# The late phases of a three-part kernel: sums of experts by accumulating DMAs, decode in whole slices, another TensorE order

## The chip, the core and the metric

One core of one Trainium2 chip. The metric is the device time of one execution in microseconds (us), the median of the runs. A core has TensorE (PE, its weight loads PEld), VectorE (DVE), ScalarE (ACT), GpSimd (POOL) and SyncE (SP), each with an instruction queue of its own that runs in order; DMAs are issued from such a queue and carried out by 16 DMA engines.

## The reference

```python
def _attn_ref(q, k, v, alpha):          # 4 batches, 8 heads, 768 steps, head width 48
    for t in range(S):
        state = alpha[:, :, t, :, None] * state + np.einsum('bhd,bhe->bhde', k[:, :, t], v[:, :, t])
        y[:, :, t] = np.einsum('bhd,bhde->bhe', q[:, :, t], state)

def _moe_ref(x, domain_probs, w1, w2):  # 3072 tokens, width 384, 4 experts of 1024
    p = domain_probs / (domain_probs.sum(-1, keepdims=True) + 1e-09)
    for e in range(E):
        h = np.maximum(x @ w1[e], 0.0)
        out += p[:, e:e + 1] * (h @ w2[e])

def _moe2_ref(x, w_in, w_out):          # hidden width 2048
    h = x @ w_in
    g = h * np.clip(h + 3.0, 0.0, 6.0) / 6.0
    return g @ w_out
```

The three run one after the other, the output of each being the x of the next. `w_in` and `w_out` arrive as 64-bit floats; everything else is 32-bit.

## The kernel before

Tokens stand in six blocks of 512 (`NB`). Matrices are held as a high and a low part in fp32r, so each product is three matmuls: high weight x high data, low x high, high x low.

**First stage, to about 460 us.** The recurrence, with the first seven weight slices (`S0` = 7, a slice is 256 columns of the hidden width) of the experts done beside it for all six blocks: all of expert 0 and three quarters of expert 1. Each block's sum for either expert is multiplied by its probability and stored in DRAM as `acc_d[0]` or `acc_d[1]`. The change leaves this stage alone; its last block ends as the "tail" (L1797).

**Second and third stage, from about 518 us.** The other nine expert slices, then the eight slices of the last layer. Here two blocks (a pair, y = 0 and 1) are worked together, and the first layer of a slice is a fast matrix product of 2 x 3 by 3 x 2 blocks in 11 products instead of 12. A *group* is one slice for one pair: 11 products (M0 to M10) and 12 second-layer units (four h tiles, `o_` = 0 to 3, by three output parts m; y = `o_` % 2). Each product and unit is three matmuls of 128x512. There are 27 groups in the second stage and 24 in the third. A *segment* is the run of groups of one expert (or of the last layer) for one pair; at its end the six sums leave PSUM. The expert segments of a pair are of 1, 4 and 4 slices, so there are nine segment ends in the second stage.

The products run in two PSUM banks. `chain_a` takes M9, M5, M0, M7, M6 in turn, `chain_b` M10, M4, M2, M3, M8, M1. Each adds to what the bank holds, and between two additions the sum so far is taken out: ScalarE copies chain_a (`ct`, add_copy, L1544), VectorE adds the copy to chain_b (`cs`, add_sum, L1552), and the gate makes an h pair (`hh`, `hl`, add_gate) of it: two steps in the second stage (L1569, L1572), four in the third (L1578 to L1583). The next product into a bank waits until that has been read: M5 and M0 and M7 for `ct`, M2, M8 and the next group's M10 for `cs`, the next M9 for the gate that reads chain_a.

**What runs beside.**
- x: `add_x` loads a pair's blocks, GpSimd forms differences (L1365 to L1379), ScalarE and VectorE split them into high and low (`X..h` L1391, `X..l` L1396).
- Weights: `add_w`; on a slice's first use two DMAs for the first layer (`f_r0`, L1443) and one for the second, GpSimd forms sums (L1463 to L1466), ScalarE casts (L1473, L1479, L1486), VectorE subtracts (L1475, L1481, L1488); the result is stored in `ws_d` and loaded from there for the other pairs.
- Decode of the 64-bit weights: `add_decode`, 48 pieces of 256 columns, 24 of `w_out` first and then 24 of `w_in`: load `draw`, VectorE L1311, ScalarE L1312, VectorE L1313 to L1325, GpSimd's add L1326, a store into `w_out32` or `w_in32`. Slices of the last layer are then loaded from these.
- Sums of experts: at a pair's first segment end VectorE multiplies the PSUM sums by the probabilities into SBUF tiles `acc` (L1675); at later ends into `o` (L1687), and GpSimd adds `o` to `acc` (L1688). GpSimd also adds what the first stage left (`acc_d[0]` and `acc_d[1]`, loaded as `xr`, L1643). When the pair is done `acc` is stored as `x2_d`, the x of the third stage.
- The end: VectorE transposes the six sums (L1712), and each is written to `out` by four DMAs of 64 KB (L1718), 18 from SP and 6 from ACT for the last pair.

**What sets the order.** All operations of the late stages are written as entries of a list, with an engine, a planned duration, a `lag` until others may use the result, and dependencies (`op`, `dma`, `dve`, `act`, `pool`, `pe_op`). TensorE's entries keep the order in which they are written. `schedule()` works due times back from them, plays the list forward, and so puts the entries of every other engine in a fixed order. That order is what is built: an engine then waits at each instruction for its semaphores, and everything behind it in its queue waits too. `Ring` objects hand out buffers in turn; who wants a buffer waits for the users of its previous content.

## Time and profile before

| | |
|---|---|
| median of 3 runs | 1354.7 us (1353.49 to 1355.38) |
| profiled execution | 1354.69 us, its span 1353.0 us, mean TensorE clock 0.991 |
| TensorE matmul busy | 1311.8 us (97% of the span) |
| VectorE, ScalarE, GpSimd busy | 981.4, 593.9, 266.2 us |
| HBM read and written | 167.69 and 70.30 MB |
| GpSimd's sums of experts (L1643, L1688) and decode adds (L1326) | 24, 36 and 48 instructions |

The span runs from the program's first instruction to its last; the profiled execution's own time is 1.7 us longer. Busy time of TensorE is modelled, since matmuls overlap, so the number of matmuls started in a stretch says more than the busy share. Names in rows are those of the program without buffer numbers: out<-in. A line is a line of the kernel before; after the change the same operations stand some 20 to 30 lines further down.

### The profile page before, as it was taken

The page shows a single profiled execution, that of the slowest core. Times are in us where ns is not written, and L with a number is a line of the kernel's source. Part 1 is how long each engine was busy: PE and PEld are TensorE (multiplying, and loading weights), DVE is VectorE, ACT ScalarE, POOL GpSimd, SP SyncE. Part 2 cuts the span into 40 slices and gives each one's busy share as a digit, 9 for nine tenths or more (in the row PEclk, how much of TensorE's full clock was granted, in tenths as well). Part 3 has the DMA queues.
Part 4 walks back from the last instruction along what each step waited for, and adds up shares of the span by engine and source line. Part 5 has one row for each costly group of instructions (what it writes and reads, how often), then busy time and mean ns, then how long its engine had stood idle before and what let it go on. Part 6 is the DMA issues. An engine that isn't in the chain of part 4 may idle for free.

```text
span 1353.0 us, 27179 instructions
## 1 busy us (share of the span) xinstructions
PE 1311.8 (97%) x10877; PEld 1087.1 (80%) x10877; DVE 981.4 (73%) x1771; ACT 593.9 (44%) x1097; POOL 266.2 (20%) x288
## 2 busy tenths in 40 slices
PE   8899999999999999989999999999999999999996
PEld 7789887888888888767877887888788888888885
DVE  8899977777875354888898879887886574455443
ACT  4655455444444233533433333334555554444442
POOL 4000000000000131448355424452540010000000
PEclk8899999999999999999999999999999999999998
DMA  7765545436252453877787678865564474446423
GB/s 205 202 169 143 166 111 144 139 95 188 76 146 64 129 195 109 281 261 266 266 288 255 201 228 277 276 215 213 195 241 159 140 202 143 145 130 166 136 74 47
DMA packets 173709, 239.76 MB, mean 177 GB/s; under 512 B 74000, under 2 KB 143504, under 8 KB 167056
## 3 DMA queue, kind: packets, MB, share of 16 engines
q1 hardware_dynamic: 170272, 237.45, 56.0%
q8 instruction: 85, 1.39, 0.4%
q10 hardware_dynamic: 3312, 0.59, 0.3%
q14 instruction: 40, 0.33, 0.1%
HBM read 167.69 MB, written 70.30 MB: 176 GB/s over the span
## 4 chain that ended last, share of the span: by engine, by line
PE 77%; DVE 9%; DMA 4%; ACT 3%; POOL 3%; issue 2%; SPq 0%; ACTq 0%; DVEq 0%; POOLq 0%
PE sum L1619 24%; PE chain_b L1534 12%; PE ph L923 12%; PE chain_a L1534 10%; PE po L969 9%; PE po L1797 2%; PE py L628 2%; PE pa L525 1%; DMA wr<-in_moe_w_dram 1%; PE py L650 1%; DMA w_out<-da 1%; PE pu L573 1%; POOL acc L1688 1%; DVE dhc L1311 1%; POOL acc L1643 1%
## 5 line engine op out<-in xcount | busy, mean ns | idle before, releaser
L1619 PE MATMUL sum<-hh,V 128*128 128x512 f32 x1224 | 377.9, 390 | 0.0
L1619 PEld LDWEIGHTS sum<-hh,V 128*128 128x128 f32 x1224 | 230.5, 188 | 48.0
L1619 PE MATMUL sum<-hl,V 128*128 128x512 f32 x612 | 238.8, 390 | 0.2 <-DVE hl L1572 0.2
L1552 DVE TENSOR_TENSOR cs<-ct,chain_b 128x512 f32<-128x512 f32 x153 | 104.6, 684 | 90.0 <-PE chain_b L1534 65.4
L1544 ACT COPY ct<-chain_a 128x512 f32<-128x512 f32 x153 | 89.5, 585 | 130.5 <-PE chain_a L1534 130.0
L1619 PEld LDWEIGHTS sum<-hl,V 128*128 128x128 f32 x612 | 115.2, 188 | 25.2 <-DVE hl L1572 0.6
L933 ACT ACTIVATE hh<-ph 128x512 fp32r<-128x512 f32 (+1 forms) x98 | 52.5, 538 | 173.9 <-PE ph L923 172.5
L937 DVE SCALAR_TENSOR_TENSOR hl<-ph,hh 128x512 fp32r<-128x512 f32 (+1 forms) x98 | 59.7, 611 | 68.1 <-ACT hh L933 67.8
L1583 DVE SCALAR_TENSOR_TENSOR hl<-g,hh 128x512 fp32r<-128x512 f32 x96 | 68.1, 709 | 55.7 <-ACT hh L1580 55.4
L1569 ACT ACTIVATE hh<-cs 128x512 fp32r<-128x512 f32 x81 | 51.2, 632 | 128.4 <-DVE cs L1552 128.3
L1370 POOL TENSOR_TENSOR pu<-room 128x256 f32<-128x256 f32 x2 | 1.6, 787 | 455.8 <-DVE X00l L1396 453.2
L969 PE MATMUL po<-hh,w1h 128*128 128x512 f32 (+1 forms) x249 | 90.5, 371 | 0.0
L1578 ACT ACTIVATE g<-cs,three 128x512 f32<-128x512 f32 x72 | 52.1, 724 | 79.7 <-DVE cs L1552 79.6
L969 PE MATMUL po<-hh,w1l 128*128 128x512 f32 (+1 forms) x249 | 86.4, 355 | 0.0
L1572 DVE SCALAR_TENSOR_TENSOR hl<-cs,hh 128x512 fp32r<-128x512 f32 x81 | 76.0, 939 | 13.8 <-ACT hh L1569 13.5
L969 PE MATMUL po<-hl,w1h 128*128 128x512 f32 (+1 forms) x249 | 80.6, 355 | 3.2 <-DVE hl L937 3.2
L923 PE MATMUL ph<-xh,w0h 128*128 128x512 f32 (+1 forms) x294 | 77.8, 374 | 2.7 <-ACT xh L893 1.2
L1580 ACT ACTIVATE hh<-g 128x512 fp32r<-128x512 f32 x96 | 60.8, 633 | 37.3 <-DVE g L1579 37.0
L1579 DVE SCALAR_TENSOR_TENSOR g<-g,cs 128x512 f32<-128x512 f32 x72 | 52.9, 735 | 33.2 <-ACT g L1578 33.1
L923 PE MATMUL ph<-xh,w0l 128*128 128x512 f32 (+1 forms) x294 | 74.6, 363 | 0.0
L923 PE MATMUL ph<-xl,w0h 128*128 128x512 f32 (+1 forms) x294 | 74.5, 362 | 0.0
L1326 POOL TENSOR_TENSOR da<-da,dhc 128x256 f32<-128x256 f32 x48 | 40.9, 852 | 167.9 <-DVE dhc L1325 106.9
(315 smaller groups left out, 2797.8 us busy)
## 6 DMA issues: line engine op xcount, KB each, us to landing
V<-ws_d SPq DMA_DIRECT2D x34, 1280.0 KB
V<-ws_d SPq DMA_DIRECT2D x34, 768.0 KB
ws_d<-V SPq DMA_DIRECT2D x17, 1280.0 KB
ws_d<-V SPq DMA_DIRECT2D x17, 768.0 KB
vl<-vd SPq DMA_DIRECT2D x96, 96.0 KB
xr<-acc_d SPq DMA_DIRECT2D x24, 384.0 KB
xr<-x_d SPq DMA_DIRECT2D x20, 384.0 KB
draw<-in_moe_w_out_dram SPq DMA_DIRECT2D x24, 256.0 KB
```

What stands on the lines that cost most here:

```text
L923: pe.matmul(ph[:, 0:n], w[:, j, fs], x[:, j, cs], start=(o == 0 and j == 0), stop=(o == 2 and j == KT - 1),)
L933: high = lambda: nc.scalar.activation(hh[:, 0:n], ph[:, 0:n], AF.Relu)
L937: nc.vector.scalar_tensor_tensor(hl[:, 0:n], ph[:, 0:n], 0.0, hh[:, 0:n].bitcast(F32), op0=ALU.max, op1=sub)
L969: pe.matmul(accs[vi][m][:, 0:n], w[:, z, ms], h[:, 0:n], **fl)
L1534: pe.matmul(chain[bank], a, b, start=first_ and o == 0, stop=o == 2, skip_group_check=True)
L1544: o = act(512, lambda: nc.scalar.copy(CR.place(k), chain[0]), dep, d)
L1552: o = dve(512, lambda: nc.vector.tensor_tensor(SR.place(k), CR[kc], chain[1], op=add), dep, oc, d)
L1572: lambda: nc.vector.scalar_tensor_tensor(HR[k][1], get(), 0.0, HR[k][0].bitcast(F32), op0=ALU.max, op1=sub),
L1579: b = dve(512, lambda: nc.vector.scalar_tensor_tensor(GR[kg], GR[kg], 6.0, get(), op0=ALU.min, op1=mul), a)
L1580: hh = act(512, lambda: nc.scalar.activation(HR.place(k)[0], GR[kg], AF.Copy, scale=1.0 / 6.0), b, d)
L1583: lambda: nc.vector.scalar_tensor_tensor(HR[k][1], GR[kg], 1.0 / 6.0, HR[k][0].bitcast(F32), op0=mul, op1=sub),
L1619: pe.matmul(bank[(y, m)], a, b, start=first_ and x == 0, stop=last_ and x == 2, skip_group_check=True)
```

## The change

1. **Sums of experts by DMA.** The tiles `acc` and GpSimd's adds go. Every segment end multiplies into `o`, and GpSimd issues a DMA that adds `o` to `acc_d[0]` in DRAM (54 of 256 KB). `acc_d[1]` is added to `acc_d[0]` block by block by six DMAs from DRAM to DRAM. `x2_d` is now `acc_d[0]` itself.
2. **Decode in whole slices.** 16 pieces of 768 columns, `w_in` and `w_out` of a slice in turn, one buffer each, the add on VectorE, the result stored in the layout in which the weights are wanted (`w32_d`). Each piece has a latest time (`cap`), 24.5 us apart.
3. **TensorE's order.** The second-layer units wait in a list, at least nine TensorE entries after their gate, and are dealt out in ones, twos and threes between the products (`seconds`).
4. **Four h pairs** instead of three (`HR`), the third of them in the pool that opens after the tail.
5. **Reserves in the list.** Entries marked `soft` (preparation of x and weights, decode, DMAs) are planned as if their inputs came later by `SOFT`: 0.2 us behind PE, 0.5 behind DVE and ACT, 1.5 behind POOL, 3 behind a DMA. The two loads of `f_r0` become one entry.
6. **Last block in halves.** In the last group the y = 0 units go first, and the last three units, of y = 1, are done in halves of 256 tokens, each with its own transposes and writes (4 writes of 32 KB instead of one set of 64 KB); of the y = 1 writes ACT issues every second one.

```diff
+    SOFT = dict(PE=200, DVE=500, ACT=500, POOL=1500, SP=3000, ON=0)
...
+    def lag(o, n_):
+        if n_.eng == o.eng and o.eng != "SP":
+            return 0
+        return o.lag + (SOFT[o.eng] if n_.soft else 0)
...
-                (n_.due - (o.lag if n_.eng != o.eng or o.eng == "SP" else 0) for n_ in o.next), default=pos + 60000
+                (n_.due - lag(o, n_) for n_ in o.next), default=pos + 60000
             ) - o.dur
-            o.due = d if o.due is None else min(o.due, d)
+            c = o.cap[0].due + o.cap[1] if isinstance(o.cap, tuple) else o.cap
+            o.due = min(x for x in (o.due, d, c) if x is not None)
...
+    w32_d = dram.tile([2 * NS2, P, 3 * SL], F32, name="w32_d")
+    x2_d = acc_d[0]
...
+    HPOOLS = (hp, hp, None, late_pool)
     HR = Ring(
-        lambda k: [(late_pool if k % 3 == 2 else hp).tile([P, 512], F32R, tag=z, name=f"{z}_{k}") for z in ("hh", "hl")], 3
+        lambda k: [(HPOOLS[k % 4] or more).tile([P, 512], F32R, tag=z, name=f"{z}_{k}") for z in ("hh", "hl")], 4
     )
...
-    AC = Ring(named("acc", [P, KT, NB], bufs=2), 2)
...
-        CW = 256
-        RAW = Ring(named("draw", [P, CW, 2], I32, bufs=2), 2)
...
+        CW = 3 * SL
+        RAW = Ring(named("draw", [P, CW, 2], I32), 1)
+        HC, SQ, A_ = (Ring(named(z, [P, CW]), 1) for z in ("dhc", "dsq", "da"))
+        for s_, y in [(s_, y) for s_ in range(NS2) for y in range(2)]:
...
-            o9 = op("POOL", 850, lambda a=a, hc=hc: nc.gpsimd.tensor_tensor(a(), a(), hc(), op=add), o8)
-            o10 = dma(350, 128, lambda a=a, d_=d_, c=c: nc.sync.dma_start(d_[:, CW * c : CW * (c + 1)], a()), o9)
+            o9 = dve(CW, lambda a=a, hc=hc: ve.tensor_tensor(a(), a(), hc(), op=add), o8, soft=True)
+            o10 = dma(350, 384, lambda a=a, x=2 * s_ + y: nc.sync.dma_start(w32_d[x], a()), o9)
...
+            for o in (o1, o2, o3, o4, o5, o6, o7, o8, o9, o10):
+                o.cap = 150000 + 24500 * (2 * s_ + y + 1)
...
-        l0 = [dma(900, 256, lambda: f_r0(0), da, dec0, later)]
-        if ph == 1:
-            l0.append(dma(500, 128, lambda: f_r0(1), da, l0[0], later))
+        l0 = [dma(1300, 384, lambda: [f_r0(x) for x in range(3 - ph)], da, dec0, later)]
...
+    def seconds(n):
+
+        nonlocal clock
+        for _ in range(n):
+            if units and units[0][0] <= clock:
+                add_unit(*units.pop(0)[1:])
+                clock += 1
+
+    def pool_dma(fn, *deps):
+
+        o = op("POOL", 1200, fn, *deps, soft=True)
+        o.lag = 5000
+        return o
+
+    def add_acc(pr, deps):
         for y in range(2):
...
+            t0 = (2 * pr + y) * NB
+            merged[2 * pr + y] = [pool_dma(lambda t0=t0, e=e: nc.gpsimd.dma_start(
+                acc_d[0][:, :, t0 : t0 + NB], acc_d[e][:, :, t0 : t0 + NB], accum_op=add), deps) for e in range(1, EP)]
...
-            o2 = pool(512, lambda: nc.gpsimd.tensor_tensor(AC[ka][:, m], AC[ka][:, m], OR[k], op=add), o1, writes[m])
+            o2 = pool_dma(lambda: nc.gpsimd.dma_start(
+                acc_d[0][:, m, b * NB : b * NB + NB], OR[k], accum_op=add), o1, merged[b])
             OR.use(k, o1, o2)
...
+        add_product(G, "M9", free_a)
+        a1 = add_copy(G, pe_last)
+        seconds(2)
         add_product(G, "M10", free_b)
+        add_product(G, "M4")
+        s0 = add_sum(G, a1, pe_last)
+        add_gate(G, 0, *s0)
+        seconds(1)
+        add_product(G, "M5", a1[1])
+        a2 = add_copy(G, pe_last)
...
+        seconds(3)
+        add_product(G, "M0", a2[1])
+        a3 = add_copy(G, pe_last)
...
+            seconds(1)
+            s3 = part_b()
+            seconds(1)
+            part_a()
...
+        seconds(2)
         add_product(G, "M8", s3[1])
+        add_product(G, "M1")
...
+        if end:
+            units.sort(key=lambda u: u[2] % 2)
+            for u in units[:-KT]:
+                add_unit(*u[1:])
+            for half in range(2):
+                for u in units[-KT:]:
+                    add_unit(*u[1:], half)
+        else:
+            seconds(2)
```

`part_b` is M2, M3, their sum and its gate, `part_a` M7, M6 and the gate that reads chain_a; before, the order was M9, M10, M4, three units, M5, M2, M3, M0, three units, M7, M6, three units, M8, M1, three units.

**Place one: TensorE, the products M5 and M0 (X12 and X14) in a group of the third stage.** `X..h` and `X..l` are the parts of x, `V..` a slice's weights, `sum` the second-layer banks. Before:

```order
L1534 MATMUL chain_a_7821<-X12h_3_12920,V00_16_13972 128x512 x2
L1534 MATMUL chain_a_7821<-X12l_3_12930,V00_16_13972 128x512
L1534 MATMUL chain_b_7822<-X17h_3_12923,V00_16_13972 128x512 x2
L1534 MATMUL chain_b_7822<-X17l_3_12935,V00_16_13972 128x512
L1534 MATMUL chain_b_7822<-X13h_3_12996,V00_16_13972 128x512 x2
L1534 MATMUL chain_b_7822<-X13l_3_13005,V00_16_13972 128x512
L1534 MATMUL chain_a_7821<-X14h_3_12937,V00_16_13972 128x512 x2
L1534 MATMUL chain_a_7821<-X14l_3_12944,V00_16_13972 128x512
```

After the change:

```order
L1553 MATMUL chain_a_7826<-X12h_3_12393,V10_17_13943 128x512 x2
L1553 MATMUL chain_a_7826<-X12l_3_12399,V10_17_13943 128x512
L1640 MATMUL sum10_7953<-hh_193_14150,V01_17_13954 128x512 x2
L1640 MATMUL sum10_7953<-hl_193_14151,V01_17_13954 128x512
L1640 MATMUL sum11_7959<-hh_193_14150,V01_17_13954 128x512 x2
L1640 MATMUL sum11_7959<-hl_193_14151,V01_17_13954 128x512
L1640 MATMUL sum12_7968<-hh_193_14150,V01_17_13954 128x512 x2
L1640 MATMUL sum12_7968<-hl_193_14151,V01_17_13954 128x512
L1553 MATMUL chain_a_7826<-X14h_3_12423,V10_17_13943 128x512 x2
L1553 MATMUL chain_a_7826<-X14l_3_12441,V10_17_13943 128x512
```

Between the product whose copy is taken and the next into the same bank stood M2 and M3 (X17, X13); now three units of the group before stand there.

**Place two: GpSimd around a segment end of the second stage.** Before:

```order
L1643 TENSOR_TENSOR acc_2_8033<-acc_2_8033,xr1_5_8652 128x3x256
L1688 TENSOR_TENSOR acc_2_8033<-acc_2_8033,o_6_8697 128x512
L1326 TENSOR_TENSOR da_5_8543<-da_5_8543,dhc_5_8535 128x256
L1643 TENSOR_TENSOR acc_2_8033<-acc_2_8033,xr0_6_8743 128x3x256
L1326 TENSOR_TENSOR da_6_8810<-da_6_8810,dhc_6_8804 128x256
```

After the change:

```order
L1482 TENSOR_TENSOR wr5_5_8592<-wr3_5_8493,wr5_5_8592 128x128
L1691 DMA acc0_d_91<-o_7_8597 128x512
L1691 DMA acc0_d_91<-o_8_8626 128x512
L1691 DMA acc0_d_91<-o_9_8643 128x512
L1691 DMA acc0_d_91<-o_10_8668 128x512
L1691 DMA acc0_d_91<-o_11_8675 128x512
L1381 TENSOR_TENSOR xr2_3_8704<-xr1_3_8599,xr0_3_8582 128x256
L1691 DMA acc0_d_91<-o_12_8692 128x512
```

The sums and the decode's adds, which stood in one queue, are gone from it; six accumulating DMAs stand there, with x and weight work between.

**Place three: VectorE at the same segment end, after the change** (`o_7` to `o_12` are the six products; `o` has four tiles):

```order
L1690 TENSOR_TENSOR o_7_8597<-sum00_7924,pp_3_8062 128x512
L1573 TENSOR_TENSOR cs_16_8611<-ct_17_8587,chain_b_7827 128x512
L1492 TENSOR_TENSOR V00_3_8594<-wr3_5_8493,V00_3_8594 128x384
L1492 TENSOR_TENSOR V00_3_8594<-wr3_5_8493,V00_3_8594 128x128
L1690 TENSOR_TENSOR o_8_8626<-sum01_7930,pp_3_8062 128x512
L1593 SCALAR_TENSOR_TENSOR hl_21_8620<-cs_16_8611,hh_21_8619 128x512
L1690 TENSOR_TENSOR o_9_8643<-sum02_7943,pp_3_8062 128x512
L1498 TENSOR_TENSOR V00_3_8594<-wr5_5_8592,V00_3_8594 128x768
L1593 SCALAR_TENSOR_TENSOR hl_22_8646<-chain_a_7826,hh_22_8645 128x512
L1573 TENSOR_TENSOR cs_17_8663<-ct_16_8564,chain_b_7827 128x512
L1690 TENSOR_TENSOR o_10_8668<-sum10_7953,pp_4_8158 128x512
L1690 TENSOR_TENSOR o_11_8675<-sum11_7959,pp_4_8158 128x512
```

`o_11` takes the tile of `o_7`, so it waits for the landing of the DMA that adds `o_7`; nine instructions lie between the two, and `V01` (the second layer's low part), `o_12` and the chain's next sum stand behind it.

## Rows read from the trace of the kernel before

**Rows 1.** Windows: us; busy (starts) of PE, PEld, DVE, ACT, POOL; PE clock; DMA; GB/s.
```profile
550.00:1000.00 450.00, 436.29 (x1890) 353.66 (x1889) 378.08 (x645) 179.10 (x354) 212.49 (x199) 1.00 0.73 247
1000.00:1325.00 325.00, 325.00 (x1436) 269.20 (x1435) 179.16 (x273) 155.88 (x259) 15.18 (x19) 1.00 0.46 144
```

**Rows 2.** Waits of TensorE from 430 us: who, for whom, total us, times, longest.
```profile
PE chain_b L1534 <- DVE cs L1552: 7.3, 8, 2.9
PE chain_a L1534 <- ACT ct L1544: 6.0, 6, 2.8
```

**Rows 3.** Time lines from 623 us: start, us, engine, instruction [idle before, released by].
```profile
624.39 1.88 POOL L1688 TENSOR_TENSOR acc<-acc,o 128x512 f32<-128x512 f32 x1
...
627.45 1.88 DVE L1311 TENSOR_SCALAR dhc<-draw 128x256 f32<-128x256 f32 x1 [0.62 <-POOL da L1326]
...
630.31 0.73 PE L1534 MATMUL chain_a<-X06h,V 128*128 128x512 f32 x2 [2.75 <-ACT ct L1544]
```

**Rows 4.** Time lines of SP and ACT around 600 us, the second piece of a weight load.
```profile
597.84 0.48 SPq L1443 DMA_DIRECT2D wr<-in_moe_w_dram  x1
...
603.76 0.71 ACT L1473 CAST V<-wr 128x384 fp32r<-128x384 f32 x2 [5.09 <-DMA wr<-in_moe_w_dram]
```

**Rows 5.** Time lines around 978 us.
```profile
977.70 1.71 POOL L1688 TENSOR_TENSOR acc<-acc,o 128x512 f32<-128x512 f32 x1
...
978.21 2.02 DVE L1481 TENSOR_TENSOR V<-wr,V 128x768 fp32r<-128x768 f32 x1
...
980.89 0.72 PE L1534 MATMUL chain_b<-X17h,V 128*128 128x512 f32 x2 [2.90 <-DVE cs L1552]
```

**Rows 6.** Groups of GpSimd's instructions from 550 to 1000 us (busy us, mean ns, idle before).
```profile
L1688 POOL TENSOR_TENSOR acc<-acc,o 128x512 f32<-128x512 f32 x36 | 53.8, 1521 | 28.5 <-DVE o L1687 28.3
L1643 POOL TENSOR_TENSOR acc<-acc,xr 128x768 f32<-128x768 f32 x24 | 44.8, 1871 | 0.5 <-DMA xr<-acc_d 0.4
L1326 POOL TENSOR_TENSOR da<-da,dhc 128x256 f32<-128x256 f32 x48 | 40.9, 852 | 167.9 <-DVE dhc L1325 106.9 <-issue 58.2 <-DMA xr<-x_d 2.9
```

**Rows 7.** Single lines on VectorE: ns least/median/most, first and last start.
```profile
L1396 DVE TENSOR_TENSOR X08l<-pu,X08h x6: 414/420/962, 471.7 to 973.3; 128x256 fp32r<-128x256 f32 x6
...
L1481 DVE TENSOR_TENSOR V<-wr,V x15: 945/959/2021, 543.6 to 1038.8; 128x768 fp32r<-128x768 f32 x15
...
L1311 DVE TENSOR_SCALAR dhc<-draw x48: 278/292/1930, 556.5 to 931.5; 128x256 f32<-128x256 f32 x48
...
L1325 DVE SCALAR_TENSOR_TENSOR dhc<-draw,dhc x48: 411/426/1401, 560.2 to 934.6; 128x256 f32<-128x256 uint32 x48
```

**Rows 8.** Groups of the page: the chain's sum and copy.
```profile
L1552 DVE TENSOR_TENSOR cs<-ct,chain_b 128x512 f32<-128x512 f32 x153 | 104.6, 684 | 90.0 <-PE chain_b L1534 65.4
L1544 ACT COPY ct<-chain_a 128x512 f32<-128x512 f32 x153 | 89.5, 585 | 130.5 <-PE chain_a L1534 130.0
```

**Rows 9.** Two 256 KB writes in a quiet stretch: SP's issue, then windows as in rows 1.
```profile
498.94 0.92 SPq L1806 DMA_DIRECT2D acc_d<-ft  x2
...
499.50:501.20 1.70, 1.70 (x9) 1.39 (x9) 0.15 (x2) 0.60 (x1) 0.00 (x0) 1.00 0.83 308
501.20:503.70 2.50, 2.50 (x13) 2.07 (x12) 0.55 (x1) 0.00 (x0) 0.00 (x0) 1.00 0.00 0
```

**Rows 10.** The end: time line, SP's writes as in rows 7, a window as in rows 1.
```profile
1338.77 11.60 SPq L1718 DMA_DIRECT2D out_dram<-end  x18
...
1340.13 0.39 PE L1619 MATMUL sum<-hl,V 128*128 128x512 f32 x1
...
L1718 SPq DMA_DIRECT2D out_dram<-end x18: 337/506/1263, 1338.8 to 1349.9; - x18
...
1342.00:1344.00 2.00, 0.00 (x0) 0.00 (x0) 0.00 (x0) 0.00 (x0) 0.00 (x0) 1.00 0.98 143
```

**Rows 11.** Time line of TensorE at 78 us: matmuls of 256 columns.
```profile
78.05 0.28 PE L969 MATMUL po<-hh,w1l 128*128 128x256 f32 x1
78.17 0.28 PE L969 MATMUL po<-hl,w1h 128*128 128x256 f32 x1
```

More of the change, by code (lines that the diff above doesn't have):

```diff
@@ L1349, in add_x @@
             ku, du = room_u.new()
-            if q == 1 and c == 0:
-                du = du + [o for us in FT.users for o in us]
             after_ = [late_ok] + x2_done.get(pr, []) * (ph == 2)
@@ L1446, in f_r0 @@
             else:
-                nc.sync.dma_start(t, src_in[:, c : c + SL].rearrange("(j p) f -> p j f", j=KT))
+                nc.sync.dma_start(rooms_w[0][ka], w32_d[2 * s_])
         def f_r1():
+            if ph == 2:
+                nc.sync.dma_start(rooms_w[1].place(kb), w32_d[2 * s_ + 1])
+                return
             nc.sync.dma_start(
@@ L1505, in add_w @@
         vq[G] = (rings, k0, k1, [h1, h3], [h5])
-    chain, sums_ = {}, {}
+    chain = {}
+    bank, bank_free = {}, {}
+    units, clock = [], 0
     free_a, free_b = [], []
@@ L1560, in add_gate @@
         if G == 0:
-            d = d + gone + ([o for us in FT.users for o in us] if k == 2 else [])
+            d = d + gone + ([o for us in FT.users for o in us] if k == 3 else []) + ([opened] if k == 2 else [])
         ks_ = None
@@ L1593, in add_gate, with add_unit @@
         hq[(G, o_)] = (k, hh, hl)
+        units.extend((clock + 9, G, o_, m) for m in range(KT))
         return reads
-    bank, bank_free = {}, {}
-    def add_second(G, o_):
+    def add_unit(G, o_, m, half=None):
         f, y = o_ // 2, o_ % 2
@@ L1606, in add_second @@
         rings, k0, k1, w0_ok, w1_ok = vq[G]
-        for m in range(KT):
-            def emit(m=m):
-                if (y, m) not in bank:
-                    pl, tag = ((ps2, "ps2"), (psa, "psa"))[y]
-                    bank[(y, m)] = pl.tile([P, 512], F32, tag=tag, name=f"sum{y}{m}")
-                wh, wl = (
-                    rings[1][k1][:, z * 3 * SL : z * 3 * SL + 3 * SL].rearrange("p (j m) -> p j m", j=2)[:, f, m * P : m * P + P]
-                    for z in range(2)
-                )
-                h, l = HR[k]
-                for x, (a, b) in enumerate(((wh, h), (wl, h), (wh, l))):
-                    pe.matmul(bank[(y, m)], a, b, start=first_ and x == 0, stop=last_ and x == 2, skip_group_check=True)
-            o = pe_op(1, emit, w1_ok, hh, hl, *(bank_free.pop((y, m), []) if first_ else []))
-            rings[1].use(k1, o)
-            HR.use(k, o)
-            if last_:
-                add_end(G, y, m, o)
@@ L1627, in tile_gla__then__moe__then__moe2 @@
[L1627 to L1648 removed]
+        ts = slice(0, NB) if half is None else slice(half * U, half * U + U)
@@ new lines, in emit @@
+        def emit():
+            if (y, m) not in bank:
+                pl, tag = ((ps2, "ps2"), (psa, "psa"))[y]
+                bank[(y, m)] = pl.tile([P, 512], F32, tag=tag, name=f"sum{y}{m}")
+            wh, wl = (
+                rings[1][k1][:, z * 3 * SL : z * 3 * SL + 3 * SL].rearrange("p (j m) -> p j m", j=2)[:, f, m * P : m * P + P]
+                for z in range(2)
+            )
+            h, l = HR[k]
+            for x, (a, b) in enumerate(((wh, h), (wl, h), (wh, l))):
+                pe.matmul(
+                    bank[(y, m)][:, ts], a, b[:, ts], start=first_ and x == 0, stop=last_ and x == 2, skip_group_check=True
+                )
@@ L1704, in add_end @@
             k, d = OR.new()
+        hs = range(2) if half is None else (half,)
+        ts = slice(hs[0] * U, hs[-1] * U + U)
         def f_turn():
-            if ends:
-                t = late_pool.tile([P, 512], F32, tag=f"X0{3 * y + m}h", name=f"end_{y}{m}")
+            if (y, m) in end_tile:
+                t = end_tile[(y, m)]
+            elif ends:
+                t = end_tile[(y, m)] = late_pool.tile([P, 512], F32, tag=f"X0{3 * y + m}h", name=f"end_{y}{m}")
             else:
@@ new lines, in add_group, with part_b, part_a @@
+        a3 = add_copy(G, pe_last)
+        def part_b():
+            add_product(G, "M2", s0[1])
+            add_product(G, "M3")
+            s3 = add_sum(G, a3, pe_last)
+            add_gate(G, 3, *s3)
+            return s3
+        def part_a():
+            nonlocal free_a
+            add_product(G, "M7", a3[1])
+            add_product(G, "M6")
+            free_a = add_gate(G, 2, None, pe_last)
+        if not end:
+            seconds(1)
+            s3 = part_b()
+            seconds(1)
+            part_a()
+        else:
+            seconds(2)
+            part_a()
+            seconds(1)
+            s3 = part_b()
```

247 lines of the change are left out of this document (103 added, 144 removed).

## The prediction

> **What bounds the kernel now.** I read the windows first. From 1000 to 1325 us TensorE never pauses and starts 1436 matmuls in 325 us, one in 0.226 us; from 550 to 1000 us it starts only 1890 in 450 us, where that pace gives 1988 [rows 1]. The 98 missing ones are 22 us. Then the waits of TensorE: all that count are products into chain_a that wait for ScalarE's copy `ct`, and into chain_b that wait for VectorE's sum `cs` [rows 2]; the two rows hold 13.3 us, and the rest of the 22 lies in pauses too short for that view and in the restart behind each pause. No row has TensorE waiting for a transfer. Last the time lines, for why copy and sum were late. Three pictures return. (a) Around 627 us a decode step on VectorE waits for the decode's add on GpSimd, which stands behind the sums of experts; the step then takes 1.88 us, and ScalarE's copy, queued behind a part of the same decode, comes 2.75 us late [rows 3]. (b) ScalarE stands 5.09 us before a cast, because the second piece of a weight load, issued at 597.84, is usable only at 603.76 [rows 4]. (c) Around 978 us a VectorE subtraction beside GpSimd's last sum takes 2.02 us, and TensorE waits 2.90 us [rows 5]. So TensorE is the bound, and what can be gained inside is these 22 us; outside there is the end, 12.6 us from TensorE's last matmul (1340.13 + 0.23 us) to the end of the span at 1353.0.
>
> **GpSimd's sums and the decode's add.** Three groups of GpSimd work go away: 53.8 + 44.8 + 40.9 = 139.5 us [rows 6], of 212.5 us in which GpSimd is busy from 550 to 1000 us [rows 1]. In their place GpSimd issues 6 accumulating DMAs between DRAM tensors and 54 from SBUF. The sums hid beside TensorE, so nothing is gained from them directly; the gain is in picture (a) and (c). That VectorE instructions with both operands in SBUF stretch while GpSimd computes is seen in their spread: 414 ns at least and 962 at most for the same 256 columns, 945 and 2021 ns for 768 [rows 7]. With two thirds of GpSimd's work gone most of that goes; the preparation of x and of the weights stays on GpSimd, and with it some of the stretching.
>
> **The decode.** Before: 48 pieces with three scalar steps of 0.29 us and three two-operand steps of 0.43 us [rows 7], 48 x 2.15 = 103 us of VectorE when undisturbed. After: 16 pieces of 768 columns, with a seventh step, the add. A 768-column two-operand step costs 0.96 us by the weight row [rows 7]; a scalar step lies between 0.29 and 0.96, I take 0.65 (0.29 / 0.43 of 0.96, the ratio of the 256-column pair). 16 x (3 x 0.65 + 4 x 0.96) = 93 us: 10 us less of VectorE, hidden beside TensorE. But one step now holds the queue for up to 0.96 us, and by the order listing the decode runs on to the fifth group of the third stage, where VectorE before is free of it.
>
> **TensorE's order.** Between the product whose copy is awaited and the next one into chain_a there were two products, now three second-layer units (place one of the order). A unit is 3 x 0.226 = 0.68 us, the copy 0.585 us and a sum 0.684 [rows 8]. The tightest reserve, ahead of M0, grows from 1.36 - 0.59 = 0.8 us to 1.4; M7 gets 5 units instead of 3, M10 five instead of four, M2 seven instead of four. M8 falls from eight to five, M9 from eight to six, which is still over 2.5 us. The stall at 630 sat at M7, the one at 980 at M2 (3 units more are 2.0 us). The list's reserves put the cast of picture (b) 10.2 us behind the load's issue, where the second piece was given 4.1; the rows show 5.9. I count the fourth h pair with this.
>
> What stays of the 22 us? From the part of it that only x's own GpSimd work explains, 1.5 us; from the crowded first groups of the third stage, 2; from the accumulating DMAs, 2.5 (next part). Sum 6; ends 1.5 (only x) and 15 (VectorE full, rival one).
>
> **The accumulating DMAs.** The ring `o` has four tiles, so the fifth and sixth product of a segment's end wait until the first and second sum has landed. Between these VectorE has some 6 us of other work (place three: three V steps, chain sums, hl), and the chain sums behind have about 2.5 us of reserve. Issue and landing together may thus take 6 us for nothing, 8 us before TensorE feels it. The trace has no such DMA. Below it: two plain 256 KB writes, the second issued by 499.9, had left the queues by 501.2 [rows 9], some 1.5 us. Above it: the 96 KB piece in the crowded stretch, 5.9 us [rows 4], with perhaps another 1 or 2 us for issue and for reading the target. I take 8 us, nearest to the crowded row, at which 9 segment ends cost about 0.3 us each.
>
> The Trainium skill speaks against this step: by "SBUF — State Buffer", box on the "DVE blocks DMA" trap under "SBUF: two separate sides", a DMA issued by GpSimd has its descriptors written by GpSimd's cores, and these are shut out while VectorE runs a scalar step in its two-port mode. The trace bears out the mode (0.29 us for the scalar step against 0.43), and no run here shows the shutting out. By that rule every accumulation may come up to one scalar step later; by the rows alone it does not, and the sum leaves it out.
>
> **The end.** Before, the first write of `out` is issued at 1338.77, 1.6 us ahead of TensorE's end, and SyncE's 18 writes take 11.60 us, 0.64 each against a median of 0.506; the DMA engines are 0.98 busy meanwhile [rows 10]. After, the y = 0 blocks are complete 6.2 us ahead of the end (nine whole units and the halves less the three last), so the first write is issued 5.3 us ahead, 3.7 us earlier. SyncE then has 24 writes instead of 18: 6 x 0.55 = 3.3 us more if a half costs what a whole does, 2.8 less than that at 0.32 for each of the 12 halves. As the transfers spread, 18 x (0.64 - 0.55) = 1.7 us of backlog go. So the gain is 3.7 - 3.3 + 1.7 = 2.1 to 4.9; I take 3. If each write costs the DMA side 11.60 / 24 = 0.48 us whatever its size, 36 take 17.4 us, and 2.1 us are lost: this is the other end. The halves themselves: 256-column matmuls start every 0.12 us [rows 11], so 18 x 0.12 - 9 x 0.226 = 0.1 us more.
>
> **Sum.** The profiled execution took 1354.69 us, the median of the runs is 1354.7, so no correction. 1354.7 - 22 + 6 - 3 + 0.1 = **1336 us**.
>
> **Rivals.**
> 1. VectorE becomes the bound at the start of the third stage: there it has 11 chain steps, weights, x and decode in a group of 15.6 us, some 13 to 15 us by the rows' shortest times, and GpSimd's x and weight work stretches some. For: the 2.02 us step lies just there [rows 5]. Against: GpSimd's last sums are gone. 15 us stay: 1354.7 - 22 + 15 - 1 = 1347.
> 2. GpSimd cannot hand out an accumulation while VectorE runs a scalar step of the decode: each is then up to 0.65 us later, at 9 ends at most 6 us: 1336 + 6 = 1342. For: these steps are the only ones of that kind in the stretch, and they now last over twice as long. Against: there are only 48 of them in 450 us. This is what the SBUF page of the Trainium skill, named above, would make of the change.
> 3. Slower: the accumulations land late. Past 8 us every us costs VectorE, and by its in-order queue TensorE, 9 us; at 8 + 18.7 / 9 = 10 us all is eaten. At 12 us: 1336 + 9 x 4 = 1372. For: a 96 KB load needed 5.9 us in that crowd. Against: nothing larger than that is seen in the rows, and the POOL queue carries no other transfers.
> 4. The change doesn't do what it says: the stalls move to other products, the end is paced by the number of writes. 22 us come back in other places: 1353 to 1356.
>
> **How the numbers follow.** Forecast 0.60 (1330 to 1341), rival 1 0.15, rival 2 0.07, better than 1330 0.03; these are faster: 0.85. Rival 4 is no change within 0.2% (2.7 us, about what a measurement of this kernel tells from nothing): 0.05. Rival 3 is slower: 0.10. The range goes from 1354.7 - 22 + 1.5 - 4.4 = 1330 (the low ends of remainder and end, the last cut by half a us) to rival 1's 1347; it holds 0.82.
>
> **What would show it.** Right: from 550 to 1000 us over 1950 matmuls; waits of TensorE for `ct` and `cs` under 5 us together; the decode's scalar step of 768 columns near 0.65 us; no VectorE `o` wait for a DMA over 2 us; the span's end 9 to 10 us behind TensorE's. Wrong: `o` waiting for `acc_d` transfers at segment ends (rival 3); VectorE over 95% busy around 960 to 1020 us with TensorE waiting there (rival 1); a last write later than 10 us behind TensorE's end.

## The result, and the profile after

Before 1354.1 us (median of four runs, 1352.8 to 1355.4), after 1336.7 us (four runs, 1332.2 to 1339.0). The ratio is 0.9867, 95% interval 0.9838 to 0.9896: faster, by 1.0 to 1.6%. The profiled execution after is the fastest of the four, 1332.18 us with a span of 1330.5 us.

The windows of [rows 1], the kernel after, from 550 to 1000 and from 1000 to 1325 us:

```profile
550.00:1000.00 450.00, 449.10 (x1982) 371.55 (x1981) 324.16 (x486) 182.72 (x337) 124.07 (x140) 1.00 0.78 243
1000.00:1325.00 325.00, 321.25 (x1426) 266.17 (x1424) 180.63 (x281) 149.73 (x255) 17.14 (x20) 1.00 0.47 152
```

1982 matmuls start where 1890 did and 1988 fit: 6 missing, 1.4 us in place of 22. (The second window is short at its end because TensorE is done at 1321.) A little is lost ahead of this window, where the kernel before lost nothing; the stretch from 460 to 550 us, before and after:

```profile
460.00:550.00 90.00, 90.00 (x399) 74.55 (x398) 51.48 (x81) 33.18 (x70) 24.24 (x30) 1.00 0.50 172
```

```profile
460.00:550.00 90.00, 87.88 (x387) 72.12 (x386) 46.60 (x75) 31.11 (x67) 26.35 (x38) 1.00 0.65 194
```

The waits of TensorE from 430 us on, in place of [rows 2]; no wait for `ct` or `cs` is left:

```profile
PE chain_a L1553 <- DVE hl L1593: 3.0, 2, 2.1
```

The time lines of VectorE, GpSimd and TensorE at the longer of these two pauses:

```profile
539.05 4.47 DVE L1593 SCALAR_TENSOR_TENSOR hl<-cs,hh 128x512 fp32r<-128x512 f32 x1
...
539.14 1.06 POOL L1381 TENSOR_TENSOR xr<-xr,xr 128x256 f32<-128x256 f32 x1
539.84 1.05 POOL L1386 TENSOR_TENSOR pu<-xr 128x256 f32<-128x256 f32 x1
540.53 1.04 POOL L1382 TENSOR_TENSOR xr<-xr 128x256 f32<-128x256 f32 x1
541.23 1.04 POOL L1383 TENSOR_TENSOR xr<-xr,xr 128x256 f32<-128x256 f32 x1
541.93 1.03 POOL L1388 TENSOR_TENSOR pu<-xr,xr 128x256 f32<-128x256 f32 x1
...
545.04 0.73 PE L1553 MATMUL chain_a<-X01h,V 128*128 128x512 f32 x2 [2.07 <-DVE hl L1593]
```

An `hl` of 0.69 us takes 4.47, because GpSimd forms x differences one right behind another; the next `hl`, which frees chain_a, is late by that, and TensorE waits 2.07 us. The other pause, of 0.90 us at 624 us, begins in the same way: an `hl` of 3.37 us at 612.22, beside x differences and a weight sum, from which VectorE works without a gap until the wait ends. GpSimd's groups from 550 to 1000 us in place of [rows 6] (first and largest arithmetic), the page's line on the accumulating DMAs (KB, median us from issue to landing), and VectorE's waits for them:

```profile
L1691 POOL DMA_DIRECT2D acc_d<-o x49 | 44.4, 978 | 197.0 <-DVE o L1690 197.0
L1483 POOL TENSOR_TENSOR wr<-wr 128x256 f32<-128x256 f32 x12 | 13.3, 1106 | 0.0
...
acc_d<-o POOLq DMA_DIRECT2D x54, 256.0 KB, 9.1
...
DVE o L1690 <- DMA acc_d<-o: 6.3, 7, 1.7
```

The decode's first step of 768 columns, in place of [rows 7]:

```profile
L1327 DVE TENSOR_SCALAR dhc<-draw x16: 547/552/1839, 549.5 to 986.9; 128x768 f32<-128x768 f32 x16
```

The end, in place of [rows 10]: SyncE's writes, TensorE's last matmul, one window:

```profile
1315.72 12.55 SPq L1725 DMA_DIRECT2D out_dram<-end  x24
...
1320.97 0.28 PE L1640 MATMUL sum<-hl,V 128*128 128x256 f32 x1
...
1322.00:1324.00 2.00, 0.00 (x0) 0.00 (x0) 0.00 (x0) 0.00 (x0) 0.00 (x0) 1.00 0.98 159
```

The span ends 9.3 us behind TensorE (1330.5 less 1321.2, the modelled end of its last matmul). Before, in the same counting, it was 12.5 us (1353.0 less 1340.5); the prediction added a matmul's step of 0.23 us instead and wrote 12.6. So the end is 3.2 us shorter.

### The profile page after: what moved, and what is told of

Read it like the earlier page. It is cut to its first block, busy times and chain, and to the rows that moved or that the text cites. A ratio compares the mean times of both kernels' runs of the same rounds, so it can differ in the third digit from the quotient of the medians.

```text
span 1330.5 us, 26800 instructions
## 1 busy us (share of the span) xinstructions
PE 1305.1 (98%) x10886; PEld 1088.2 (82%) x10886; DVE 914.7 (69%) x1598; ACT 583.7 (44%) x1065; POOL 185.8 (14%) x240
## 4 chain that ended last, share of the span: by engine, by line
PE 89%; DVE 4%; ACT 2%; issue 1%; DMA 1%; SPq 0%; POOL 0%; DVEq 0%; ACTq 0%; POOLq 0%
PE sum L1640 30%; PE chain_b L1553 15%; PE ph L923 12%; PE chain_a L1553 12%; PE po L969 10%; PE po L1830 2%; PE py L628 2%; PE pa L525 2%; PE py L650 1%; PE pu L573 1%; PE py L611 1%; ACT qt L481 1%; DMA acc_d<-o 1%; DVE hl L937 0%; DVE kt L513 0%
## 5 line engine op out<-in xcount | busy, mean ns | idle before, releaser
L1640 PE MATMUL sum<-hh,V 128*128 128x512 f32 (+1 forms) x1230 | 377.2, 388 | 0.0
L1640 PE MATMUL sum<-hl,V 128*128 128x512 f32 (+1 forms) x615 | 238.6, 388 | 0.0
L937 DVE SCALAR_TENSOR_TENSOR hl<-ph,hh 128x512 fp32r<-128x512 f32 (+1 forms) x98 | 59.6, 610 | 75.4 <-ACT hh L933 72.7
L1593 DVE SCALAR_TENSOR_TENSOR hl<-cs,hh 128x512 fp32r<-128x512 f32 x81 | 67.9, 839 | 29.9 <-ACT hh L1590 29.5
L1691 POOL DMA_DIRECT2D acc_d<-o x54 | 48.6, 974 | 208.4 <-DVE o L1690 208.3
L923 PEld LDWEIGHTS ph<-xh,w0h 128*128 128x128 f32 x294 | 50.5, 191 | 12.4 <-DVE hl L937 3.3
```

Of the source, the lines that this page charges most:

```text
L923: pe.matmul(ph[:, 0:n], w[:, j, fs], x[:, j, cs], start=(o == 0 and j == 0), stop=(o == 2 and j == KT - 1),)
L937: nc.vector.scalar_tensor_tensor(hl[:, 0:n], ph[:, 0:n], 0.0, hh[:, 0:n].bitcast(F32), op0=ALU.max, op1=sub)
L1593: lambda: nc.vector.scalar_tensor_tensor(HR[k][1], get(), 0.0, HR[k][0].bitcast(F32), op0=ALU.max, op1=sub),
L1640: pe.matmul(bank[(y, m)][:, ts], a, b[:, ts], start=first_ and x == 0, stop=last_ and x == 2, skip_group_check=True)
```

## Experiments

"Missing" counts matmul starts from 550 to 1000 us against 1988, times 0.226 us. Their window rows are those of [rows 1]. In each, TensorE's work is the same, but for the halves at the end.

**The change once more** (`again`), no edit.

> The changed kernel once more, unaltered. Its four runs lie between 1332.2 and 1339.0 us, and the profiled one was the fastest, with TensorE pausing twice in the late phases for 3.3 us, both times behind an hl on VectorE that GpSimd's x work stretched to 3.4 and 4.5 us. Theory (the rest of the stalls has one source, GpSimd arithmetic beside two-operand VectorE work, and varies with its timing): median 1335 to 1338, and a run of 1336 shows 3 to 5 us more of such pauses between 520 and 1020 us. Rival (the spread comes from the first stage): the late phases look as before, and TensorE starts the second stage later by 3 to 5 us.

Measured: 1334.8 us (1333.2 to 1337.5), ratio 0.9856 [0.9842, 0.9871]. The profiled run, at 1333.2, has the same two pauses (2.6 us). So the pauses repeat; but this profile is not of an execution of 1336 us, in which the theory put 3 to 5 us more of them. What differs between executions shows in other profiles. The first product of the second stage starts at 517.30 us in the change's profile, at 518.64 in this one, and at 519.36 to 522.78 in four of the runs below (`end_old` 519.36, `soft0` 521.05, `dec_old` 521.70, `order_old` 522.78), which alter nothing in the first stage. That is the rival, and it is good for up to 5.5 us. But not all is that: in `end_old`, whose late phases are those of the change up to the last group, the pause of 2.07 us is followed by more than 3 us at a granted clock of 0.50 (the 1.2 GHz level), and in the change by none. The window rows of 3 us behind that pause, the change first, then `end_old`:

```profile
546.20:549.20 3.00, 3.00 (x15) 2.48 (x14) 2.73 (x5) 1.83 (x6) 2.70 (x4) 1.00 1.04 436
```

```profile
548.30:551.30 3.00, 3.00 (x9) 2.33 (x8) 2.33 (x4) 1.77 (x6) 2.74 (x4) 0.50 1.02 425
```

**Accumulating DMAs alone** (`b_dma`), in the kernel before.

```diff
-            o2 = pool(512, lambda: nc.gpsimd.tensor_tensor(AC[ka][:, m], AC[ka][:, m], OR[k], op=add), o1, writes[m])
+            o2 = pool_dma(lambda: nc.gpsimd.dma_start(
+                acc_d[0][:, m, b * NB : b * NB + NB], OR[k], accum_op=add), o1, merged[b])
```

> The kernel before with the sums of experts alone done by accumulating DMAs. Theory (GpSimd's sums caused most late decode steps and stretched subtractions): GpSimd loses 99 us of work, the waits of TensorE for ct and cs fall from 13 us to 4 to 7, 1342 to 1347. Rival one (the late second piece of the weight load and the old order set the pauses): 1350 to 1355. Rival two (the sums wait for landings of 9 us and hold VectorE back): over 1356.

Measured: 1368.7 us (1364.2 to 1371.3), ratio 1.0101 [1.0083, 1.0119]: slower. The theory fell. The window row, and TensorE's waits:

```profile
550.00:1000.00 450.00, 428.65 (x1845) 350.01 (x1844) 330.46 (x636) 174.92 (x348) 148.10 (x182) 0.98 0.79 240
```

```profile
PE chain_b L1533 <- DVE cs L1551: 13.1, 6, 3.9
PE chain_a L1533 <- ACT ct L1543: 9.6, 4, 4.2
```

143 are missing, 32 us, though GpSimd is busy for 148 us instead of 212. The waits hold 22.7 us of it; behind pauses the granted clock falls as well (0.72 in the mean from 562 to 568 us, 0.62 from 712 to 721). The time lies in rival two's range (over 1356), but not by its cause: VectorE waits for landings of `o` for 6.8 us in all. The time lines of two of the pauses show what came late:

```profile
617.87 0.48 SPq L1442 DMA_DIRECT2D wr<-in_moe_w_dram  x1
...
627.47 0.71 ACT L1472 CAST V<-wr 128x384 fp32r<-128x384 f32 x2 [6.43 <-DMA wr<-in_moe_w_dram]
...
712.47 0.51 DVE L1310 TENSOR_SCALAR dhc<-draw 128x256 f32<-128x256 f32 x1 [5.00 <-DMA draw<-in_moe_w_out_dram]
```

Loads: the second piece of a weight load is usable 9.6 us behind its issue (5.9 in [rows 4]), and a decode load holds VectorE's queue for 5.0 us. From 618 to 628 us, around the first, the DMA share is 1.07, where it was 0.67 before in the same stretch, and a third of the DMA engines' time is that of the queue that only the accumulations use. The stretch before, then here, and that queue's share here:

```profile
618.00:628.00 10.00, 9.55 (x43) 7.54 (x41) 6.82 (x7) 3.61 (x7) 9.84 (x9) 1.00 0.67 227
```

```profile
618.00:628.00 10.00, 7.37 (x33) 5.73 (x31) 5.01 (x12) 1.95 (x5) 1.81 (x3) 1.00 1.07 344
q0 software_dynamic: 357, 0.63, 34.3%
```

So the accumulations take a share of busy DMA engines and the loads beside them land later; that the fixed order of the list had no room for this is what `b_dma_soft` tests below.

**Reserves alone** (`b_soft`), in the kernel before (with the weight load as one entry, and with the tail's third result made to wait, in the list, for the x differences in its tile).

```diff
-                (n_.due - (o.lag if n_.eng != o.eng or o.eng == "SP" else 0) for n_ in o.next), default=pos + 60000
+                (n_.due - lag(o, n_) for n_ in o.next), default=pos + 60000
```

> The kernel before with the reserves alone and the weight load as one entry: GpSimd's sums, decode in 48 pieces, old TensorE order and old end stay. Theory (GpSimd's arithmetic and late loads each make about half of the 21 us of pauses, and reserves heal only the loads): pauses of 6 to 12 us, 1340 to 1348. Rival one (reserves heal all, the accumulating DMAs were not needed): 3 to 6 us as with DMAs and reserves together, 1336 to 1341. Rival two (reserves only heal the harm of the accumulating DMAs): 18 us or more, 1350 to 1356.

Measured: 1360.0 us (1356.5 to 1363.5), ratio 1.0039 [1.0025, 1.0054]. By the number none of the three, since it has one new pause that the others lack: at 483 us, in the tail, TensorE waits 13.9 us for `ft`, because the tail's third result shares a tile with x's differences there, and in the list's new order these come first. The change gives it a tile of its own. Behind that pause:

```profile
PE chain_b L1540 <- DVE cs L1558: 4.0, 5, 1.9
PE sum L1625 <- DVE hl L1589: 1.0, 1, 1.0
```

```profile
550.00:1000.00 450.00, 445.00 (x1954) 365.70 (x1953) 361.41 (x617) 182.92 (x356) 200.58 (x186) 1.00 0.71 238
```

34 missing, 7.7 us, with GpSimd's sums still there (200.6 us). So two thirds of the 22 us go by the list alone (the reserves and the single load entry, which were not tried apart), as the theory's 6 to 12 had it; VectorE and ScalarE wait for no load from 530 to 1030 us. (The window lies 14 us earlier in the work than in the others.)

**Both together** (`b_dma_soft`): the two edits above, and a tile of its own for the tail.

> The kernel before with the accumulating DMAs and the reserves, the weight load as one entry and a tile of its own for the tail's third result, all else as before: old TensorE order, decode in 48 pieces with GpSimd's add, three h pairs, old end. Theory (the reserves turn the loss of 33 us with the DMAs alone into a gain): pauses of 4 to 10 us, 1338 to 1346. Rival (the old order or the old decode makes the pauses, whatever the reserves): 25 us or more of them, 1357 to 1368.

Measured: 1340.9 us (1339.5 to 1342.6), ratio 0.9903 [0.989, 0.9916]; as the theory had it.

```profile
550.00:1000.00 450.00, 447.89 (x1968) 368.58 (x1969) 343.90 (x656) 189.83 (x374) 155.28 (x188) 1.00 0.82 250
```

20 missing, 4.5 us. Adding the reserves to the DMAs takes 27.7 us off (1368.7 less 1340.9); by the windows' counts the DMAs are good for some 3 us with reserves (7.7 to 4.5), and cost 10 without (22 to 32). Even with the old TensorE order, three h pairs and the decode in 48 pieces, little is left for the rest of the change to gain inside.

**The order alone** (`b_order`), in the kernel before: the change's order in all groups, the last one included, with three h pairs and whole units.

```diff
-        m9 = add_product(G, "M9", free_a)
-        a1 = add_copy(G, m9)
+        end = False
+        add_product(G, "M9", free_a)
+        a1 = add_copy(G, pe_last)
+        seconds(2)
         add_product(G, "M10", free_b)
```

> The kernel before with the new TensorE order alone, three h pairs, the last group in the same order and its units whole. Theory (longer stretches between a product and the next into its bank cover copies and sums that are up to 2 us late): pauses of 8 to 14 us in place of 21, 1341 to 1349. Rival (with three h pairs the units, which now come nine places behind their gate, hold the pairs, and the gates wait): 18 to 30 us, 1350 to 1363.

Measured: 1419.1 us (1416.0 to 1421.9), ratio 1.0475 [1.0459, 1.0491]. The rival, and far worse. TensorE's waits:

```profile
PE chain_a L1535 <- DVE hl L1575: 32.1, 27, 1.4
PE chain_a L1535 <- ACT ct L1547: 24.2, 24, 1.3
```

and what ScalarE waited for from 530 to 1030 us:

```profile
ACT hh L1572 <- PE sum L1623: 240.7, 84, 6.3
```

The gate's `hh` waits for the units that still read the pair; behind it stand the copy and the next gate. With four pairs the same wait after the change is 59.6 us, 42 times, and costs TensorE nothing. In this kernel the fourth pair is no addition to the order but its condition; the change with three pairs was not run.

**The old order** (`order_old`), in the kernel after (last group as changed).

```diff
+            add_gate(G, 0, *s0)
+            if G:
+                three(G - 1, 2)
+            add_product(G, "M5", a1[1])
...
+                three(G - 1, 1)
+            add_product(G, "M7", a3[1])
```

> The changed kernel with the old TensorE order in all groups but the last: units in threes, M2 and M3 ahead of M0, M8 behind units of the same group. Theory (the causes of late copies and sums are mostly gone, the new order covers what stays): 4 to 10 us of pauses for ct and cs come back, 1341 to 1347. Rival one (the order alone removed the 22 us): 1352 to 1358. Rival two (the order does nothing once GpSimd is quiet): 1334 to 1339.

Measured: 1336.4 us (1334.6 to 1340.4), ratio 0.9861 [0.9846, 0.9877], against 0.9856 of the change on the same chip: rival two.

```profile
550.00:1000.00 450.00, 448.34 (x1973) 369.64 (x1972) 317.53 (x477) 182.91 (x334) 119.87 (x140) 1.00 0.79 244
```

In its window 1973 start, 9 fewer than after the change (2 us); its waits for `cs` and `ct` are 3.2 us. Of the 8.2 us by which its profiled run (1340.4) is longer than the change's, 5.5 are the late start named above. The order is worth 0 to 4 us here.

**No reserves** (`soft0`), in the kernel after.

```diff
-    SOFT = dict(PE=200, DVE=500, ACT=500, POOL=1500, SP=3000, ON=0)
+    SOFT = dict(PE=0, DVE=0, ACT=0, POOL=0, SP=0, ON=0)
```

> The changed kernel with all of the list's reserves at zero. Theory (accumulating DMAs make loads late, as the kernel before with them alone showed, and the reserves keep late loads off the engines' queues): pauses of TensorE behind ct, cs or hl of 10 to 25 us between 520 and 1020 us, 1342 to 1358. Rival (the new order and the fourth h pair cover late loads anyway): pauses of 3 to 6 us, 1333 to 1339.

Measured: 1343.5 us (1339.4 to 1347.4), ratio 0.9919 [0.9904, 0.9934]: the theory's side, at its low end.

```profile
550.00:1000.00 450.00, 443.88 (x1943) 364.77 (x1942) 333.44 (x488) 180.15 (x333) 126.27 (x147) 1.00 0.80 249
```

1943 start, 45 missing, 10 us against 1.4. (The profiled runs of this and of the next kernel also started the second stage 3.8 and 4.4 us later than the change's, so the windows are a safer measure here than the times.) Here the rival of the prediction that ends slower is seen at work, in small:

```profile
PE sum L1640 <- DVE o L1690: 4.1, 3, 1.8
```

```profile
DVE o L1690 <- DMA acc_d<-o: 15.4, 8, 4.7
```

VectorE waits 15.4 us for landings, up to 4.7 at a time, where the change with its reserves waits 6.3 and at most 1.7.

**Decode in small pieces, add on GpSimd** (`dec_old`), in the kernel after.

```diff
-            o9 = dve(CW, lambda a=a, hc=hc: ve.tensor_tensor(a(), a(), hc(), op=add), o8, soft=True)
...
+                p9 = pool(256, lambda a=a, hc=hc, w=w: nc.gpsimd.tensor_tensor(a()[:, w], a()[:, w], hc()[:, w], op=add), p8, soft=True)
```

> The changed kernel with each decode slice worked in three pieces of 256 columns and the add on GpSimd again; loads, stores and latest times as changed. Theory (the decode's add on GpSimd is one of the causes of late work): GpSimd has 41 us more, VectorE's decode steps wait for it, 3 to 8 us more of pauses, 1338 to 1343. Rival (with the sums gone the add does no harm, and smaller steps hold VectorE's queue for less time): 1332 to 1337.

Measured: 1343.9 us (1340.9 to 1346.2), ratio 0.9924 [0.991, 0.9937]. The theory's upper end: 7 to 9 us for the decode's form, some of which may be the later start.

```profile
550.00:1000.00 450.00, 445.60 (x1954) 367.06 (x1953) 324.66 (x633) 180.39 (x361) 157.66 (x184) 1.00 0.78 239
```

34 starts are missing in the window (7.7 us against 1.4, some of it from the granted clock, 0.50 from 551 to 554 us behind the first pause), and TensorE waits 1.3 us at 995 us, inside it, and 1.4 us at 1017 us, behind it, in the first groups of the third stage. Which of the two does it, the pieces or GpSimd's add, was not tried apart. Nor is this a fixed price: `b_dma_soft`, with 48 pieces and GpSimd's add, lost only 4.5 us in its window.

**GpSimd's arithmetic on VectorE** (`dve_all`), in the kernel after: differences of x and sums of weights; GpSimd then only issues DMAs.

```diff
-            tt = nc.gpsimd.tensor_tensor
+            tt = nc.vector.tensor_tensor
...
-        p0 = pool(2 * P, lambda: (rooms_w[2].place(kc), tt(
+        p0 = dve(2 * P, lambda: (rooms_w[2].place(kc), tt(
```

> The changed kernel with the x differences and the weight sums on VectorE instead of GpSimd, so that GpSimd only issues DMAs in the late phases. Theory (what stalls are left is GpSimd arithmetic beside VectorE): no hl over 0.9 us, no pause of TensorE over 1 us behind hl, 1329 to 1333 and a narrower spread. Rival (VectorE has no room: 122 of 150 us busy from 550 to 700, and some 55 us more work in all): pauses for cs at 550 to 700 and around 960 to 1020 us, 1338 to 1350.

Measured: 1330.2 us (1329.7 to 1331.2), ratio 0.9821 [0.9808, 0.9835]: faster than the change, as the theory had it. TensorE has no wait left in the late phases.

```profile
550.00:1000.00 450.00, 450.00 (x1987) 372.69 (x1986) 324.96 (x567) 181.64 (x337) 41.99 (x48) 1.00 0.78 243
```

GpSimd loses 82 us of work, VectorE has 81 instructions more, and VectorE's busy time is the same (324.96 against 324.16 us): what it took over costs what the stretching had cost. `hl` from `cs` is at 688 ns in the mean, where it was 797 in the same window.

**The end.** `end_old` is the kernel after without sort and without halves; `dve_whole` and `dve_end` are the kernel above, the first without halves, the second without both.

```diff
-            units.sort(key=lambda u: u[2] % 2)
-            for u in units[:-KT]:
-                add_unit(*u[1:])
-            for half in range(2):
-                for u in units[-KT:]:
-                    add_unit(*u[1:], half)
+            for u in units:
+                add_unit(*u[1:])
```

> The changed kernel with its last group's units in the order of their gates and whole, so that the y = 1 sums are not cut in halves and y = 0 is not done first. Theory: TensorE ends where it does in the changed kernel, the span 12 to 13 us later instead of 9.3, so 3 us more: 1337 to 1340. Rival (the number of writes paces the end, so fewer of them give back what the later start costs): the same end within 1 us, 1333 to 1337.

> The changed kernel with GpSimd's differences and sums on VectorE, and the last block's units whole, y = 0 still first. Theory (24 writes fewer in number and larger end sooner than 36, as the kernel with the old end showed): the span ends 8.3 to 8.7 us behind TensorE instead of 9.3, 1329 to 1330. Rival (halves are what lets the last transfers start early): 10 us or more, 1331 to 1334.

> The same with the last group's units whole and in the order of their gates, y = 0 not put first. Theory (the end gains from the two gates of y = 0 standing first, not from the sort): 8.3 to 8.7 us behind TensorE as with the sort, 1329 to 1330. Rival (without the sort the y = 0 writes start later by up to 2 us): 9.5 to 11 us, 1331 to 1333.

Measured: `end_old` 1336.4 us (1331.3 to 1338.7, ratio 0.9865 [0.9847, 0.9882]); `dve_whole` 1328.2 us (1326.8 to 1331.9, 0.9809 [0.9794, 0.9823]); `dve_end` 1329.0 us (1327.9 to 1334.3, 0.9826 [0.9806, 0.9846]). By time the three lie inside each other's spread with their partner, so I read the distance from TensorE's end to the span's end in the profiles: 9.3 us with sort and halves (the change, and `dve_all`), 8.5 and 8.4 without both, 8.0 with the sort alone. SyncE's writes of `end_old` and its last line on them:

```profile
1321.57 9.98 SPq L1725 DMA_DIRECT2D out_dram<-end  x18
...
L1725 SPq DMA_DIRECT2D out_dram<-end x18: 316/488/523, 1321.6 to 1331.0; - x18
```

and the latter for the change:

```profile
L1725 SPq DMA_DIRECT2D out_dram<-end x24: 315/456/518, 1315.7 to 1327.8; - x24
```

So my expectation for `end_old` (12 to 13 us) fell. The gain of the end needs neither halves nor sort. What is left of the change there is that the products M7 and M6, and with them the second gate of y = 0, stand ahead of M2 and M3 in the last group. `b_order` has the new order without this swap. Its last write and matmul lines:

```profile
1402.47 11.77 SPq L1722 DMA_DIRECT2D out_dram<-end  x18
...
1404.70 0.39 PE L1623 MATMUL sum<-hl,V 128*128 128x512 f32 x1
```

Its span ends at 1417.0, 11.9 us behind TensorE. Side by side, in us; the lead is the time from the first write to TensorE's end:

| kernel | last group | SyncE's writes | lead | first write to span's end | TensorE's end to span's end |
|---|---|---|---|---|---|
| before | old order | 18 | 1.8 | 14.2 | 12.5 |
| `b_order` | new order, no swap | 18 | 2.6 | 14.5 | 11.9 |
| `end_old`, `dve_end` | swap | 18 | 4.7 | 13.1 | 8.5, 8.4 |
| `dve_whole` | swap, sort | 18 | 5.3 | 13.3 | 8.0 |
| the change, `dve_all` | swap, sort, halves | 24 | 5.5 | 14.8 | 9.3 |
| `order_old` | the same behind the old order | 24 | 6.9 | 14.7 | 7.8 |

The lead sets most of it. From `b_order` to `end_old` it grows by 2.0 us, which is the three units (3 x 0.68) that the swap puts behind the y = 0 sums. That the swap is the cause is borne out by this and not shown alone: `b_order` is otherwise the kernel before, so it also lacks the fourth h pair, the reserves and the latest time (`cap`) that the change gives the last transposes and writes. Halves lose about 1 us (9.3 against 8.0): a write of half the size occupies SyncE nearly as long (459 ns median in `dve_all`, 491 in `dve_whole`), and there are six more.

The lowest median of all is that of `dve_whole`, 1.9% under the kernel before and below the change; against `dve_all` its interval does not part it.

## Why the prediction was right, and where its working was not

The time was forecast at 1336 and came at 1336.7, inside 1330 to 1341. By its steps:

- **What bounds the kernel**: right. The 22 us of pauses went to 4.1 (1.4 from 550 to 1000 us, and 2.7 from the time before that: 387 starts from 460 to 550 us where 399 were). With the end's 3.2 us, and a second stage that started 1.3 us earlier, that comes to the 1332.2 of the profiled execution; the median of the runs is 4.5 us above that profile, so part of the agreement with 1336 is chance. What the prediction called the restart behind each pause is in part the granted clock: before, it is 0.50 from 632 to 634 us, behind the pause at 630.
- **"What stays of the 22 us"**: 6 forecast, 4.1 measured, but of another make. GpSimd's own work, which the prediction set at 1.5 us and as x's alone, is all of it (at the second pause a weight sum stands in it too); the 2 us for the first groups of the third stage and the 2.5 us for accumulations are not there.
- **"GpSimd's sums and the decode's add ... the gain is in picture (a) and (c)"**: this step failed. Taking the sums away alone cost 14.5 us, and leaving them in place with the reserves took 14 of the 22 us of pauses away. GpSimd's contention is real (without its arithmetic TensorE has no wait left), but most of what it cost came from a list that planned each input for the moment it was wanted. The prediction used the list's reserves for picture (b) only.
- **"The tightest reserve, ahead of M0, grows from 1.36 - 0.59 = 0.8 us to 1.4"** and **"I count the fourth h pair with this"**: these stretches between a product and the next into its bank (not the list's reserves) are longer as worked out, and bought 0 to 4 us. The fourth pair was priced at nothing, without a reason, where with three the order costs the kernel before 65 us.
- **The accumulating DMAs**: landing 9.1 us (4.0 to 14.2) where 8 was taken. By the third rival's rule, 9 us for every us past 8, that would be 10 us. It cost none: VectorE waited seven times, 1.7 us at most, and the chain's sums had the room. What the step left out is the other side: the same transfers delay loads, by 3.7 us for one weight piece in the kernel with them alone. Four of the six DMAs from DRAM to DRAM are issued in the first stage, from 169.3 us on, so the change does not leave that stage quite alone.
- **The decode**: 0.55 us for a scalar step of 768 columns where 0.65 was taken; its form is worth some 6 to 9 us inside the change. The prediction counted its time on VectorE as hidden and the add on GpSimd with picture (a); which of the two it is stays open.
- **The end**: 3 forecast, 3.2 measured, and the first write 5.5 us ahead where 5.3 was worked out. The bound "if a half costs what a whole does" was nearly the right one. Most of the earlier start came with the swap of products (2.9 of the 3.8 us without sort and halves), and the halves gave some of it back.
- **Rivals**: VectorE was never the bound (69% busy from 850 to 1100 us). The second rival costs nothing that shows: the accumulations' issues take 0.87 us at the median, and no wait of TensorE hangs on one. Whether a scalar step holds one up is open; the median landing is 8.1 us with steps of 256 columns (`dec_old`), and with steps of 768 it is 9.1 in the change and 7.8 in `order_old`. The slower rival shows at 4.1 us without reserves, and as one wait of TensorE of 1.3 us in `end_old`, behind an `o` that had waited 2.0 us for a landing; in the change there is none.

## What to carry to other kernels

Where a planner fixes the order of in-order queues, a planned lag is a promise: put a margin on every entry that is not urgent before adding traffic, because the same accumulating DMAs cost 14 us without margins and gained a little with them. Try the parts of a bundle singly in both directions, since here the DMAs, the reserves and the order each made the kernel before slower when they came alone (the reserves by a shared tile), and the bundle gained 1.3%. Arithmetic on GpSimd is not free help when VectorE works on two SBUF operands beside it: moved to VectorE it cost no busy time there.

## What the runs showed of the hardware that was not expected

- One VectorE instruction can lose a whole run of GpSimd instructions: `hl` began at 539.05 us, five GpSimd instructions ran from 539.14 to 542.96, and it ended at 543.52, some 0.6 us behind the last. The Trainium skill, "SBUF — State Buffer", section "Who interferes with whom", says that a VectorE instruction with two SBUF inputs contends with one of GpSimd that reads SBUF. The rows agree; that the wait goes on over several instructions is what the rows add.
- The same pause of 2.07 us was followed by the lower clock level in one execution (granted 0.50, the 1.2 GHz level, from 548.3 to 551.3 us in `end_old`) and by none in another (1.00 in the change), with the same instructions ahead.
- Accumulating DMAs of 256 KB land 4.0 to 14.2 us behind their issue in the crowded stretch, and in the change VectorE waited 6.3 us for them in all and TensorE not at all; without reserves their price was paid by the loads beside them (9.6 us for a 96 KB piece, against 5.9).
